# Last rows' attention scores as four 64x64 products, later pairs' scores in three float32r passes, and one PSUM pool kept for both phases

## Chip, core, metric

One core of one Trainium2 chip runs the whole program: an attention block and two mixture-style feed-forward layers, all in float32. The metric is the device time of one execution in microseconds. Engine names are those of the profile: PE is TensorE, PEld its weight loads, DVE VectorE, ACT ScalarE, POOL GpSimd, SP the engine that issues most DMAs.

## What is computed

```
# q, k, v: (4, 8, 576, 64); s: (4, 8, 576)
scores = scale * q @ k.T
cum = cumsum(max(s, 0));  bias = -(cum[:, None] - cum[None, :])
scores = where(causal, -1e9, scores + min(bias, 0))
scores -= max(scores);  attn = exp(scores);  attn /= sum(attn) + 1e-9
x = (attn @ v) as 2304 tokens x 512
h = x @ w1_in;  x = max(0.01 * h, h) @ w1_out        # 512 -> 2048 -> 512
h = x @ w2_in;  out = softplus(h) @ w2_out           # 512 -> 2048 -> 512
```

The causal mask leaves only keys at or before the query, where the bias is never above 0, so `min(bias, 0)` changes nothing that counts. The term `-cum[query]` is the same for a whole row and falls away when the row's maximum is taken off; only `+cum[key]` matters to the result, up to a constant of the row.

## The kernel before

**Attention.** Thirty-two (batch, head) maps are worked off as 16 pairs of heads `p` (four pairs per batch). Head 0 of a pair lies on partitions 0 to 63 of `Q`, `K` and so on, head 1 on partitions 64 to 127. The 576 queries are four blocks of 128 rows (`t` = 0 to 3) and a rest of `TL` = 64 rows. A pair has four units, in this order: block 3 (512 keys), the last 64 rows (all 576 keys, written `[]`), block 2 (384 keys), and blocks 1 and 0 together (256 and 128 keys).

`Unit.scores` makes the scores on PE. For the blocks, each product is made per head on 64 partitions (the two heads use the upper and lower half of the array's rows): a float32 product of `Q` and `K`, then a float32r product of `BQ` and `BK`, whose few non-zero rows hold the running sums `cum` in two parts and so add the decay (L286). For the last rows, both heads go through the whole array at once (L276): `Q` carries the 64 rows of head 0 and head 1 side by side with zeros in between, so that 128 output rows come out, in two halves of 288 keys, each a float32 product and a float32r decay product. The first pair has its decay in float32 (`BQ0`, `BK0`, shown as `PB` in the trace).

Then, per unit and head: `maxima` on DVE adds the mask and finds the row maximum (L305); `exps` on ACT (L319); `divisors` on DVE (L325, L326); `norm` on POOL (L330); `transpose` on PE (L347; the last rows L342 and L338); `evacuate` on ACT (L359) or DVE (L361); and `pv` on PE, which multiplies by V, the two heads on the two halves of the array's columns (L378), split into `xh` and `xl` on ACT and DVE (L385, L389).

The loop over units is written out by hand: in step `n`, scores of unit `n+1`, maxima and exponentials of `n`, norms of `n-1`, transposes of `n-2`. `i` is the step within a pair. Each engine takes its instructions in program order. `tick` and `later` put small follow-up work some half steps on.

**Fill.** From the second batch on, PE gets other work in between: `Fill` makes the first of four slices of the first layer for the tokens that are ready, in three chunks of `FW` = 512 columns (L143 and L583), half a unit per step, and stores the partial result (`part`). It also loads and splits weights (`load_w`, `split_w`: three DVE, three ACT and two POOL instructions each, L106 to L131), some of them in the first batch already.

**Feed-forward.** Every float32 product is made of three float32r products of high and low parts (`h_mm` L143, `out_mm` L709). The rest of the first slice goes over `first`, two chunks of 384 columns. After attention the PSUM pool `psA` closes, and the pools `ps_o` and `ps_h` open in its place. Stores and loads between the phases are on SP's queue, in program order.

Of the kernel before, what the change touches and what calls it, by code (L numbers as in the profile page):

```python
# [2 lines left out]

# [14 lines left out]
P = 128  # L18
# [12 lines left out]
def attn_moe_moe(ctx, tc, q, k, v, s, w1i, w1o, w2i, w2o, out):  # L31
# [12 lines left out]
    TL = S - NB * P  # L44
    FW = 512
    scale = 1.0 / float(D) ** 0.5
# [12 lines left out]
    xl = keep.tile([P, KD, NT], F32R, tag="xl", name="xl")  # L59
    bb_d = dram.tile([B * H, 2, S], F32R, tag="bb_d", name="bb_d")  # L60
    part = dram.tile([B - 1, P, KD, FW], F32, tag="part", name="part")

# [90 lines left out]
    def attention(att, ps, fills):  # L153
# [3 lines left out]

        ZQ = NB * P + 2 * TL
        own = [[slice(0, NB * P + TL)], [slice(0, NB * P), slice(NB * P + TL, ZQ)]]
        two = lambda nm, shape, dt=F32: [att.tile(shape, dt, tag=f"{nm}{i}", name=f"{nm}{i}") for i in range(2)]  # L160
        Q, K = two("Q", [P, ZQ]), two("K", [P, S])
        BQ, BK = two("BQ", [P, ZQ], F32R), two("BK", [P, S], F32R)
        V = two("V", [P, NB + 1, 2, D])
# [12 lines left out]
        def blank(i):  # L176

            bq = BQ[i].bitcast(F32)
            nc.gpsimd.memset(bq, 0.0)
            for j in range(2):  # L180
                for c in own[j]:
                    nc.gpsimd.memset(bq[j * D:j * D + 2, c], 1.0)

        def wake(x):

            pt = ps.tile([P, 512], F32, tag="a", name="pt_w", bufs=1)
            for i in range(8):
                nc.tensor.matmul(pt[:, :P], x, x, start=True, stop=True)

        def decay0():  # L190

            pitch = list(s1.ap[0])[0]
            nc.sync.dma_start(
                bass.AP(s1.tensor, s1.offset, [[D * pitch, 2], [1, S]]), bass.AP(s.tensor, s.offset, [[S, 2], [1, S]])
            )
            load(0, "q", nc.scalar)
            nc.sync.dma_start(c0, s.rearrange("b h s -> (b h) s"))
            load(0, "k", nc.scalar)
# [12 lines left out]
            nc.scalar.activation(BQ0[32:33, :S], BK0[:1], AF.Copy)  # L211
            n = 0
            for c, queue in zip(own[1], (nc.vector, nc.gpsimd)):
                m = n + c.stop - c.start
                queue.tensor_copy(BQ0[D + 32:D + 33, c], BK0[D:D + 1, n:m])
                n = m

# [6 lines left out]
        def parts():  # L224
            nc.vector.tensor_tensor(lo.bitcast(F32R), c1, hi, op=ALU.subtract)
            for e, x in enumerate((hi, lo)):
                nc.sync.dma_start(bb_d[:, e, :].bitcast(F32), x)

        def zeros():
# [5 lines left out]

        def load(p, nm, queue=nc.sync):
            if p < NP:
                t, x = {"q": (Q, q), "k": (K, k), "v": (V, v)}[nm]
                queue.dma_start(t[p % 2], x[p])

        def rows(p):

            if p < NP:
                b, hs = heads(p)
                for j in range(2):
                    h, r = b * H + hs.start + j, j * D
                    move(BK[p % 2][r:r + 2], bb_d[h])
                    n = 0
                    for c in own[j]:
                        m = n + c.stop - c.start  # L250
                        move(BQ[p % 2][r + 32:r + 34, c], bb_d[h, :, n:m])
                        n = m


        class Unit:
            def __init__(self, p, ts):
                self.p, self.ts = p, ts
                self.last = not ts
                o = 0
                self.subs = []  # L260
                for t in ts:
                    self.subs.append((t, slice(o, o + (t + 1) * P)))
                    o += (t + 1) * P
                self.W = S // 2 if self.last else o
                self.n = 1 if self.last else 2 * len(ts)

            def scores(self):
                i = self.p % 2
                bq, bk = (BQ[i], BK[i]) if self.p else (BQ0, BK0)
                ops = (Q[i], K[i]), (bq, bk)  # L270
                self.ps = [ps.tile([P, 512], F32, tag=f"s{j}", name="pt_s", bufs=2) for j in range(2)]
                if self.last:

                    for j, pt in enumerate(self.ps):
                        for x, y in ops:
                            nc.tensor.matmul(  # L276
                                pt[:, :self.W], x[:, NB * P:], y[:, j * self.W:(j + 1) * self.W],
                                start=x is Q[i], stop=x is bq,
                            )
                    return  # L280

                for t, c in self.subs:
                    for x, y in ops:
                        for j in range(2):
                            r = slice(j * D, (j + 1) * D)
                            nc.tensor.matmul(  # L286
                                self.ps[j][:, c], x[r, t * P:(t + 1) * P], y[r, :(t + 1) * P],
                                start=x is Q[i], stop=x is bq,
                            )
# [4 lines left out]
            def maxima(self, j):  # L294
                if j == 0:
# [4 lines left out]
                w = slice(0, self.W)  # L300
                todo = [(w, (mask[:, w], maskl)[j], j)] if self.last else [
                    (c, mask[:, (NB - 1 - t) * P:], j * len(self.subs) + i) for i, (t, c) in enumerate(self.subs)
# [120 lines left out]
        decay()  # L423
        fill.step(-2)
        load(1, "q")
        load(1, "k")
# [12 lines left out]
        for n in range(len(units) + 3):  # L439
# [48 lines left out]
    class Fill:  # L488
        def __init__(self, ps):
# [15 lines left out]
            def begin():  # L505

                with_o.__exit__(None, None, None)
                self.gpool, self.tpool = new("gpoolA", G + 1), new("tpoolA", 2)

# [39 lines left out]
        def h(self, f, x, gs):  # L549
            ps = self.bank("ps_h")  # L550
            h_mm(ps, 0, f, *x, range(KD // 2))
            new = lambda pool, nm, dt=F32: pool.tile([P, FW], dt, tag=nm, name=nm)

            def leaky():
                gf = new(self.tpool, "gf")
                nc.scalar.activation(gf, ps, AF.Prelu, alpha=0.01)
                later(1, high, gf)
# [17 lines left out]
        def o(self, dm, c, gs):  # L575
            ps = self.bank("ps_o")
            w = slice(dm * P, (dm + 1) * P)
# [18 lines left out]

    with pool("psA", bufs=2, space=PSUM) as psA:
        fills = []

        def make():  # L600
            fills.append(Fill(psA))
            return fills[0]

        with pool("att") as att:
            attention(att, psA, make)
        fill = fills[0]
        while fill.units or fill.rest or todo:
            fill.run()
            tick()
        fill.stack.close()  # L610

# [80 lines left out]
    def out_mm(n):  # L692
# [6 lines left out]
        for i in range(n_out):  # L699
            if f == 0:  # L700
                outs[i] = ps_o.tile([P, 512], F32, tag="o", name="ps_out")
        for i in range(n_out):
# [44 lines left out]
    for n, (layer, g, c, is_first, is_last, f) in enumerate(steps):  # L747
        N = c[1]
        cols = slice(c[0], c[0] + N)
        ps = ps_h.tile([P, 512], F32, tag="h", name="ps_h")  # L750
        h_mm(ps[:, :N], layer, g * G + f, xh[:, :, cols], xl[:, :, cols])
# [18 lines left out]
def lay_out(name, a):  # L770
# [9 lines left out]
    if name == "v":  # L780
# [3 lines left out]
        return r  # L784
    r = np.zeros((B * H // 2, 2, D, S + (tl if name == "q" else 0)), a.dtype)
    r[..., :S] = a.transpose(0, 1, 3, 2)
    if name == "q":
        r[:, 1, :, S:] = r[:, 1, :, n * P:S]
        r[:, 1, :, n * P:S] = 0
    return r.reshape(-1, 2 * D, r.shape[-1])  # L790

# [19 lines left out]
```

## Time and profile before

| | us |
|---|---|
| median of three runs | 986.3 (the others 985.24 and 1078.37) |
| the profiled execution | 985.13 |
| its span | 983.4 |
| PE busy | 973.2 (99%) |
| PE weight loads busy | 797.1 (81%) |
| DVE / ACT / POOL busy | 529.2 / 537.6 / 568.5 |
| chain that ended last: PE's share | 95% |

Attention fills the first quarter of the span, to about 254 us; the rest is feed-forward. A PE instruction's listed time holds its latency, and the next one starts while it runs, so what a piece of work costs PE is read from start to start. A float32 product stands as two records in the trace, a float32r product as one. The granted TensorE clock is 1.00 in every window.

### The profile page before, as it was taken

The page shows a single profiled execution, that of the slowest core. Times are in us where ns is not written, and L with a number is a line of the kernel's source. Part 1 is how long each engine was busy: PE and PEld are TensorE (multiplying, and loading weights), DVE is VectorE, ACT ScalarE, POOL GpSimd, SP SyncE. Part 2 cuts the span into 40 slices and gives each one's busy share as a digit, 9 for nine tenths or more (in the row PEclk, how much of TensorE's full clock was granted, in tenths as well). Part 3 has the DMA queues.
Part 4 walks back from the last instruction along what each step waited for, and adds up shares of the span by engine and source line. Part 5 has one row for each costly group of instructions (what it writes and reads, how often), then busy time and mean ns, then how long its engine had stood idle before and what let it go on. Part 6 is the DMA issues. An engine that isn't in the chain of part 4 may idle for free.

```text
span 983.4 us, 14578 instructions
## 1 busy us (share of the span) xinstructions
PE 973.2 (99%) x5226; PEld 797.1 (81%) x5226; DVE 529.2 (54%) x1139; ACT 537.6 (55%) x1119; POOL 568.5 (58%) x553
## 2 busy tenths in 40 slices
PE   8999999999999999999999999999999999999998
PEld 5767777777898888888888888888888888888886
DVE  7976666555121322232226347767587858764434
ACT  6887667656454333334335456776656555654452
POOL 7766456444264455345535546777777777874554
PEclk9999999999999999999999999999999999999999
DMA  6322331310540111011101210112011101100202
GB/s 200 123 102 81 125 122 63 111 52 25 178 134 22 52 56 43 22 48 60 43 22 44 65 43 22 43 44 64 23 44 43 59 27 44 44 1 1 86 22 86
DMA packets 35239, 61.20 MB, mean 62 GB/s; under 512 B 2566, under 2 KB 19718, under 8 KB 35168
## 3 DMA queue, kind: packets, MB, share of 16 engines
q1 hardware_dynamic: 34736, 59.53, 18.4%
q8 instruction: 41, 0.67, 0.3%
q10 hardware_dynamic: 432, 0.75, 0.2%
q14 instruction: 30, 0.25, 0.1%
HBM read 52.26 MB, written 8.01 MB: 61 GB/s over the span
## 4 chain that ended last, share of the span: by engine, by line
PE 95%; DVE 2%; ACT 1%; POOL 1%; issue 0%; DMA 0%; DVEq 0%; ACTq 0%; POOLq 0%
PE ps_h L143 40%; PE ps_out L709 37%; PE pt_v L378 4%; PE pt_s L286 4%; PE pt_t L347 3%; PE ps_o L583 3%; PE pt_s L276 2%; PE pt_t L342 1%; POOL sc L330 1%; ACT sc L319 1%; DVE sc L305 0%; DMA sc<-in_s 0%; POOL wm L121 0%; DVE acc L724 0%; DVE wm L118 0%
## 5 line engine op out<-in xcount | busy, mean ns | idle before, releaser
L149 POOL TENSOR_TENSOR gl<-gf,gh 128x512 fp32r<-128x512 f32 (+2 forms) x148 | 183.1, 1237 | 151.3 <-ACT gh L148 141.7
L143 PE MATMUL ps_h<-xh,wih 128*128 128x512 f32 (+2 forms) x640 | 237.7, 371 | 0.7 <-ACT o L587 0.7
L143 PE MATMUL ps_h<-xh,wil 128*128 128x512 f32 (+2 forms) x640 | 235.7, 368 | 0.0
L143 PE MATMUL ps_h<-xl,wih 128*128 128x512 f32 (+2 forms) x640 | 235.7, 368 | 0.0
L724 DVE TENSOR_TENSOR acc<-ps_out,acc 128x512 f32<-128x512 f32 (+1 forms) x115 | 73.8, 658 | 164.1 <-PE ps_out L709 164.1
L674 POOL TENSOR_TENSOR t<-e,t 128x512 f32<-128x512 f32 (+1 forms) x80 | 112.3, 1404 | 72.1 <-DVE t L673 71.3
L330 POOL TENSOR_SCALAR sc<-sc,st 128x512 f32<-128x512 f32 (+4 forms) x160 | 87.6, 560 | 96.7 <-DVE st L326 83.5
L143 PEld LDWEIGHTS ps_h<-xh,wih 128*128 128x128 f32 x640 | 120.6, 188 | 20.4 <-ACT o L587 1.2
L143 PEld LDWEIGHTS ps_h<-xh,wil 128*128 128x128 f32 x640 | 120.5, 188 | 19.6
L143 PEld LDWEIGHTS ps_h<-xl,wih 128*128 128x128 f32 x640 | 120.7, 189 | 19.1
L658 ACT ACTIVATE gf<-ps_h 128x512 f32<-128x512 f32 (+2 forms) x68 | 37.2, 547 | 178.1 <-PE ps_h L143 174.1
L148 ACT ACTIVATE gh<-gf 128x512 fp32r<-128x512 f32 (+2 forms) x148 | 86.1, 581 | 49.2 <-DVE gf L684 48.5
L709 PE MATMUL ps_out<-woh,gl 128*128 128x512 f32 x288 | 112.4, 390 | 0.0
L709 PE MATMUL ps_out<-woh,gh 128*128 128x512 f32 x288 | 112.3, 390 | 0.0
L709 PE MATMUL ps_out<-wol,gh 128*128 128x512 f32 x288 | 112.3, 390 | 0.0
L121 POOL TENSOR_TENSOR wm<-wm,wt 128x512 int32<-128x512 int32 x64 | 84.9, 1327 | 30.7 <-DVE wm L118 30.7
L319 ACT ACTIVATE sc<-sc,st 128x512 f32<-128x512 f32 (+2 forms) x144 | 83.5, 585 | 29.4 <-DVE st L325 22.8
L709 PE MATMUL ps_out<-gh,wol 128*128 128x512 f32 (+2 forms) x272 | 99.1, 364 | 0.0
L709 PE MATMUL ps_out<-gh,woh 128*128 128x512 f32 (+2 forms) x272 | 99.1, 364 | 0.0
L709 PE MATMUL ps_out<-gl,woh 128*128 128x512 f32 (+2 forms) x272 | 99.0, 364 | 0.0
L673 DVE TENSOR_SCALAR t<-e 128x512 f32<-128x512 f32 (+1 forms) x80 | 44.3, 553 | 98.4 <-ACT e L664 98.4
L112 DVE TENSOR_SCALAR wm<-wm 128x512 f32<-128x512 f32 x64 | 38.3, 599 | 95.6 <-ACT wm L106 95.4
(107 smaller groups left out, 1704.9 us busy)
## 6 DMA issues: line engine op xcount, KB each, us to landing
rawi<-in_moe_w_in SPq DMA_DIRECT2D x32, 512.0 KB
rawo<-in_moe_w_out SPq DMA_DIRECT2D x32, 512.0 KB
V<-in_v SPq DMA_DIRECT2D x16, 320.0 KB
Q<-in_q SPq DMA_DIRECT2D x15, 320.0 KB
out<-acc SPq DMA_DIRECT2D x17, 256.0 KB
K<-in_k SPq DMA_DIRECT2D x15, 288.0 KB
part<-o SPq DMA_DIRECT2D x12, 256.0 KB
acc<-part SPq DMA_DIRECT2D x3, 1024.0 KB
```

What stands on the lines that cost most here:

```text
L121: nc.gpsimd.tensor_tensor(m, m, t, op=ALU.add)
L143: nc.tensor.matmul(ps, a, b, start=kk == 0 and n == 0, stop=kk == KD - 1 and n == 2)
L148: nc.scalar.activation(gh, gf, AF.Copy)
L149: nc.gpsimd.tensor_tensor(gl, gf, gh.bitcast(F32), op=ALU.subtract)
L286: nc.tensor.matmul(self.ps[j][:, c], x[r, t * P:(t + 1) * P], y[r, :(t + 1) * P], start=x is Q[i], stop=x is bq,)
L319: nc.scalar.activation(x, x, AF.Exp, scale=-1.0, bias=self.stat(0, e), accum_out=self.stat(1, e))
L330: nc.gpsimd.tensor_scalar(x, x, self.stat(2, e), 1.0, op0=ALU.mult, op1=ALU.mult)
L378: nc.tensor.matmul(pt[j * D:(j + 1) * D, o:o + w], V[p % 2][:, c, j, :], x[:, j, :], start=m == 0 or (not last and m == 1), stop=m == len( ...
L673: nc.vector.tensor_scalar(t, e, 1.0, -1.0, op0=ALU.add, op1=ALU.add)
L674: nc.gpsimd.tensor_tensor(t, e, t, op=ALU.subtract)
L709: nc.tensor.matmul(ps, a, b, start=f == 0 and m == 0, stop=f == G - 1 and m == 2)
L724: nc.vector.tensor_tensor(d[..., x], o[..., x], d[..., x], op=ALU.add)
```

## The change

Five edits that hang together:

- **Last rows.** `Q` no longer holds zeros; the 64 last queries of the two heads are stored a second time with the heads swapped, and so are 288 keys of each head in `K` (864 columns now, 576 before). The scores are four float32 products of 64 rows by 64 columns of the array and 288 keys, one per quadrant of the array, with no decay product except for the first pair.
- **Decay of the last rows by DVE.** `decays` loads `cum` of the two heads, spread over 64 partitions each, into `M` (a DMA of 128 x 576 and one of 128 x 1, from the new DRAM tile `c_d`); `bias` takes off one column and adds the mask's 64 columns. `M` then stands in the place of the mask in `maxima`.
- **Three passes.** From pair index 7 on, blocks 3, 2 and 1 are made of three float32r products (`QH KH`, `QH KL`, `QL KH`) in place of one float32 product. `split` makes the parts a pair ahead: per operand one ACT copy and one DVE subtraction of 128 x 512.
- **Chunks of 448** columns in the fill, and `first` becomes two chunks of 480; some fill pools have one buffer fewer.
- **PSUM pool kept.** `psA` stays open; the feed-forward phase takes its banks by name (three for `ps_h`, five for `ps_out`, as many as before).

Also: the loads of `Q` and `K` are issued a step earlier in the pair and two pairs ahead, the decay rows (`rows`) come in four DMAs of 512 columns, not five, and the program starts with 12 dummy products, not 8.

```diff
-    FW = 512
+    FW = 448
...
-            for i in range(8):
+            for i in range(12):
...
+        def decays(p):
+
+            if p < NP:
+                o = c_d.offset + p * 2 * S
+                nc.sync.dma_start(M[:, :S], bass.AP(c_d.tensor, o, [[S, 2], [0, D], [1, S]]))
+                nc.sync.dma_start(M[:, S:S + 1], bass.AP(c_d.tensor, o + SB, [[S, 2], [1, TL], [1, 1]]))
+
+        def bias(p):
+            if 0 < p < NP:
+                nc.vector.tensor_scalar(M[:, :S], M[:, :S], M[:, S:S + 1], None, op0=ALU.subtract)
+                nc.vector.tensor_tensor(M[:, SB:S], M[:, SB:S], maskl[:, SH - TL:], op=ALU.add)
+
+
+        PARTS = 2 * NPAIR - 1
+
+        def split(p, h, l, x):
+
+            if PARTS <= p < NP:
+                h, l, x = h[p % 2], l[p % 2], x[p % 2][:, :SB]
+                nc.scalar.activation(h, x, AF.Copy)
+                later(1, lambda: nc.vector.tensor_tensor(l, x, h.bitcast(F32), op=ALU.subtract))
...
-                ops = (Q[i], K[i]), (bq, bk)
+                ops = [(Q[i], K[i]), (bq, bk)]
+                few = [(QH[i], KH[i]), (QH[i], KL[i]), (QL[i], KH[i]), (bq, bk)] if self.p >= PARTS else ops
...
-                    for j, pt in enumerate(self.ps):
-                        for x, y in ops:
+                    for e in range(2):
+                        for j, pt in enumerate(self.ps):
+                            r, o = (slice(h * D, (h + 1) * D) for h in (j, j ^ e))
+                            x, y = (S, S) if e else (SB, j * SH)
                             nc.tensor.matmul(
-                                pt[:, :self.W], x[:, NB * P:], y[:, j * self.W:(j + 1) * self.W],
-                                start=x is Q[i], stop=x is bq,
+                                pt[o, :SH], Q[i][r, x:x + TL], K[i][r, y:y + SH], start=True, stop=self.p > 0
+                            )
+                    if not self.p:
+                        for j, pt in enumerate(self.ps):
+                            nc.tensor.matmul(
+                                pt[:, :SH], bq[:, SB:], bk[:, j * SH:(j + 1) * SH], start=False, stop=True
                             )
...
-                    for x, y in ops:
+                    for m, (x, y) in enumerate(few if t else ops):
...
             if i == 0:
+                bias(p)
                 if p:
-                    load(p + 1, "q")
-                    load(p + 1, "k")
                     rows(p + 1)
+            elif i == 1:
+                split(p + 1, QH, QL, Q)
+            elif i == 2:
+                split(p + 1, KH, KL, K)
+                decays(p + 1)
+            else:
+                load(p + 2, "q")
+                load(p + 2, "k")
...
-    with pool("psA", bufs=2, space=PSUM) as psA:
-        fills = []
...
+    psA = ctx.enter_context(pool("psA", bufs=2, space=PSUM))
+    fills = []
...
-    ps_o = ctx.enter_context(pool("ps_o", bufs=5, space=PSUM))
-    ps_h = ctx.enter_context(pool("ps_h", bufs=3, space=PSUM))
+    banks = {
+        "ps_h": cycle((("t", 2), ("t", 2), ("a", 1))),
+        "ps_out": cycle((("m", 1), ("s0", 2), ("s0", 2), ("s1", 2), ("s1", 2))),
+    }
```

PE's order at pair index 8, from block 3's scores to the last rows' scores; `pt_s` are scores, `pt_t` transposes of an earlier unit, `ps_o` fill. Before:

```order
L286 MATMUL pt_s<-K_86,Q_84 128x512 x2
L286 MATMUL pt_s<-BK_90,BQ_88 128x512 x2
L342 MATMUL pt_t<-ident,sc 128x128 x4
...
L338 MATMUL pt_t<-ident,sc 64x128
L276 MATMUL pt_s<-K_86,Q_84 128x288
L276 MATMUL pt_s<-BK_90,BQ_88 128x288
L276 MATMUL pt_s<-K_86,Q_84 128x288
L276 MATMUL pt_s<-BK_90,BQ_88 128x288
```

Now, at the same place:

```order
L311 MATMUL pt_s<-KH_98,QH_94 128x512 x2
L311 MATMUL pt_s<-KL_100,QH_94 128x512 x2
L311 MATMUL pt_s<-KH_98,QL_96 128x512 x2
L311 MATMUL pt_s<-BK_91,BQ_89 128x512 x2
L368 MATMUL pt_t<-ident,sc 128x128 x4
...
L364 MATMUL pt_t<-ident,sc 64x128
L297 MATMUL pt_s<-K_87,Q_85 64x288 x4
```

Two float32 products of block 3 became six float32r products, and the four products of the last rows over the whole array became four over a quarter of it each; the neighbours are the same.

DVE's order at pair index 7, from the end of block 3's maxima to block 2's; `pt_t` copies are evacuations, `xl` belongs to `pv`. Before:

```order
L326 RECIPROCAL st<-st 128x4
L305 ISA sc,st<-pt_s,mask 128x512
...
L389 TENSOR_TENSOR xl<-pt_v,xh 128x192
L305 ISA sc,st<-pt_s,maskl 128x288
...
L361 COPY PB<-pt_t 128x3x128
L305 ISA sc,st<-pt_s,mask 128x384
...
L326 RECIPROCAL st<-st 128x1
L305 ISA sc,st<-pt_s,mask 128x384
```

Now, at the same place:

```order
L352 RECIPROCAL st<-st 128x4
L260 TENSOR_SCALAR M<-M 128x576
L261 TENSOR_TENSOR M<-M,maskl 128x64
L331 ISA sc,st<-pt_s,mask 128x512
...
L415 TENSOR_TENSOR xl<-pt_v,xh 128x192
L271 TENSOR_TENSOR QL_96<-Q_85,QH_94 128x512
L331 ISA sc,st<-pt_s,M 128x288
...
L352 RECIPROCAL st<-st 128x1
L271 TENSOR_TENSOR KL_100<-K_87,KH_98 128x512
L331 ISA sc,st<-pt_s,mask 128x384
```

Each of the three steps has new DVE work ahead of the second head's maxima: two instructions of `bias` in every pair but the first, and one subtraction in each of two steps from pair index 6 on.

## Rows read from the trace of the kernel before

**Rows 1.** The page: busy us of each engine, share of the span, instructions.
```profile
PE 973.2 (99%) x5226; PEld 797.1 (81%) x5226; DVE 529.2 (54%) x1139; ACT 537.6 (55%) x1119; POOL 568.5 (58%) x553
```
**Rows 2.** Who PE waited for, whole span: us in total, times, longest us.
```profile
PE pt_t L347 <- POOL sc L330: 1.0, 3, 0.5
PE ps_h L143 <- ACT o L587: 0.7, 1, 0.7
```
**Rows 3.** Windows of one pair each: length, busy us of PE, PEld, DVE, ACT, POOL, clock, DMA.
```profile
28.89:39.67 10.78, 10.78 (x94) 7.94 (x92) 10.37 (x41) 9.99 (x30) 8.58 (x13) 1.00 0.42 142
39.67:50.44 10.77, 10.77 (x93) 7.95 (x92) 9.58 (x39) 9.33 (x26) 7.58 (x12) 1.00 0.41 139
50.44:62.97 12.53, 12.05 (x94) 8.25 (x92) 11.24 (x39) 9.92 (x30) 8.10 (x12) 1.00 0.24 79
...
79.30:95.64 16.34, 16.34 (x117) 12.26 (x116) 10.68 (x38) 12.32 (x32) 12.13 (x16) 1.00 0.23 78
...
110.61:126.94 16.33, 16.33 (x117) 12.25 (x116) 10.03 (x39) 10.74 (x29) 8.20 (x13) 1.00 0.39 125
```
**Rows 4.** The chain of waits in the first 64 us: start, us, what.
```profile
26.86 0.66 PE pt_t L347 x4
...
46.71 0.49 ACT PB L359
...
60.93 0.66 PE pt_t L347 x4
```
**Rows 5.** PE's timeline, first pair, float32 decay of the last rows: start, us, what.
```profile
8.44 0.65 PE L276 MATMUL pt_s<-PB 128*128 128x288 f32 x2
8.92 0.65 PE L276 MATMUL pt_s<-K,Q 128*128 128x288 f32 x2
```
**Rows 6.** PE's timeline, feed-forward, twelve float32r products of 512 columns.
```profile
300.09 0.39 PE L709 MATMUL ps_out<-gh,woh 128*128 128x512 f32 x1
...
302.81 0.39 PE L143 MATMUL ps_h<-xh,wih 128*128 128x512 f32 x1
```
**Rows 7.** PE's timeline of one pair: block 3, the last rows, and what follows each.
```profile
190.89 1.13 PE L286 MATMUL pt_s<-K,Q 64*128 64x512 f32 x4
...
192.18 0.66 PE L342 MATMUL pt_t<-ident,sc 128*128 128x128 f32 x4
...
194.16 0.65 PE L276 MATMUL pt_s<-K,Q 128*128 128x288 f32 x2
...
195.41 0.49 PE L347 MATMUL pt_t<-ident,sc 128*128 128x128 f32 x3
```
**Rows 8.** The timeline of the same pair: `pv` of 192 columns, then block 2.
```profile
197.54 1.52 PE L378 MATMUL pt_v<-PA,V 128*64 128x192 f32 x16
...
199.10 0.92 PE L286 MATMUL pt_s<-K,Q 64*128 64x384 f32 x4
...
200.13 0.55 PE L347 MATMUL pt_t<-ident,sc 128*128 128x128 f32 x3
```
**Rows 9.** Single lines: duration in ns, min/median/max, then first and last start.
```profile
L112 DVE TENSOR_SCALAR wm<-wm x64: 410/428/1365, 10.9 to 873.0; 128x512 f32<-128x512 f32 x64
L310 DVE TENSOR_TENSOR st<-st x16: 158/612/1307, 12.7 to 233.0; 128x1 f32<-128x1 f32 x16
L646 DVE TENSOR_TENSOR xl<-acc,xh x20: 411/684/1778, 519.1 to 599.4; 128x512 fp32r<-128x512 f32 x16, 128x256 fp32r<-128x256 f32 x4
L125 ACT ACTIVATE wih<-wm x32: 617/632/636, 16.9 to 862.8; 128x512 fp32r<-128x512 f32 x32
```
**Rows 10.** The timeline of DVE and ACT in one pair's step of block 2.
```profile
187.23 0.62 ACT L319 ACTIVATE sc<-sc,st 128x384 f32<-128x384 f32 x1 [1.59 <-DVE st L325]
...
187.32 0.54 DVE L305 CUSTOM_DVE_ANT_0 sc<-pt_s,mask 128x384 f32<-128x384 f32 x1
```
**Rows 11.** The timeline from attention to feed-forward, on DVE and PE.
```profile
253.84 0.56 DVE L389 TENSOR_TENSOR xl<-pt_v,xh 128x384 fp32r<-128x384 f32 x1 [4.20 <-ACT xh L385]
...
255.58 0.44 PE L143 MATMUL ps_h<-xh,wih 128*128 128x384 f32 x1 [0.74 <-ACT o L587]
```

More of the change, by code (lines that the diff above doesn't have):

```diff
@@ L2 @@
 from contextlib import ExitStack
+from itertools import cycle
 import concourse.bass as bass
@@ L154, in attention @@
         ident = att.tile([P, P], F32, tag="ident", name="ident")
-        ZQ = NB * P + 2 * TL
-        own = [[slice(0, NB * P + TL)], [slice(0, NB * P), slice(NB * P + TL, ZQ)]]
+        SB, SH = NB * P, S // 2
+        ZQ, ZK = S + TL, S + SH
         two = lambda nm, shape, dt=F32: [att.tile(shape, dt, tag=f"{nm}{i}", name=f"{nm}{i}") for i in range(2)]
-        Q, K = two("Q", [P, ZQ]), two("K", [P, S])
-        BQ, BK = two("BQ", [P, ZQ], F32R), two("BK", [P, S], F32R)
+        Q, K = two("Q", [P, ZQ]), two("K", [P, ZK])
+        BQ, BK = two("BQ", [P, SB], F32R), two("BK", [P, SB], F32R)
+        M = att.tile([P, S + 32], F32, tag="M", name="M")
+        QH, QL, KH, KL = (two(nm, [P, SB], F32R) for nm in ("QH", "QL", "KH", "KL"))
         V = two("V", [P, NB + 1, 2, D])
@@ L197, in decay0 @@
             nc.sync.dma_start(c0, s.rearrange("b h s -> (b h) s"))
-            load(0, "k", nc.scalar)
+            load(0, "k", nc.scalar, slice(0, S))
             nc.vector.memset(one[:, :P], 1.0)
@@ L211, in decay0 @@
             nc.scalar.activation(BQ0[32:33, :S], BK0[:1], AF.Copy)
[L212 to L216, printed above, removed]
+            for c, n, queue in ((slice(0, SB), 0, nc.vector), (slice(S, ZQ), SB, nc.gpsimd)):
+                queue.tensor_copy(BQ0[D + 32:D + 33, c], BK0[D:D + 1, n:n + c.stop - c.start])
         hi, lo = one[:BH], c0
@@ L246, in rows @@
                     h, r = b * H + hs.start + j, j * D
[L247 to L252, printed above, removed]
+                    move(BK[p % 2][r:r + 2], bb_d[h, :, :SB])
+                    move(BQ[p % 2][r + 32:r + 34], bb_d[h, :, :SB])
+        def decays(p):
[13 more added lines that the diff above has]
+                later(1, lambda: nc.vector.tensor_tensor(l, x, h.bitcast(F32), op=ALU.subtract))
         class Unit:
@@ L263, in __init__ @@
                     o += (t + 1) * P
-                self.W = S // 2 if self.last else o
+                self.W = SH if self.last else o
                 self.n = 1 if self.last else 2 * len(ts)
@@ L300, in maxima @@
                 w = slice(0, self.W)
-                todo = [(w, (mask[:, w], maskl)[j], j)] if self.last else [
+                ml = (mask[:, w], maskl)[j] if not self.p else M[:, j * SH:(j + 1) * SH]
+                todo = [(w, ml, j)] if self.last else [
                     (c, mask[:, (NB - 1 - t) * P:], j * len(self.subs) + i) for i, (t, c) in enumerate(self.subs)
@@ L424, in attention @@
         fill.step(-2)
+        load(0, "k", nc.sync, slice(S, None))
         load(1, "q")
@@ L507, in begin @@
                 with_o.__exit__(None, None, None)
[L508 removed]
+                self.gpool, self.tpool = new("gpoolA", G), new("tpoolA", 2)
             self.begin = begin
@@ L549, in h @@
         def h(self, f, x, gs):
-            ps = self.bank("ps_h")
+            ps = self.bank("ps_h")[:, :FW]
             h_mm(ps, 0, f, *x, range(KD // 2))
@@ L554, in leaky @@
             def leaky():
-                gf = new(self.tpool, "gf")
+                gf = self.tpool.tile([P, FW], F32, tag="gf", name="gf", bufs=1)
                 nc.scalar.activation(gf, ps, AF.Prelu, alpha=0.01)
@@ L575, in o @@
         def o(self, dm, c, gs):
-            ps = self.bank("ps_o")
+            ps = self.bank("ps_o")[:, :FW]
             w = slice(dm * P, (dm + 1) * P)
@@ L595, in o, with make @@
             self.rest = rest
-    with pool("psA", bufs=2, space=PSUM) as psA:
-        fills = []
[L600 to L610, printed above, removed]
+    psA = ctx.enter_context(pool("psA", bufs=2, space=PSUM))
+    fills = []
+    def make():
+        fills.append(Fill(psA))
+        return fills[0]
+    with pool("att") as att:
+        attention(att, psA, make)
+    fill = fills[0]
+    while fill.units or fill.rest or todo:
+        fill.run()
+        tick()
+    fill.stack.close()
     wpools.append(ctx.enter_context(pool("wpool1", bufs=2)))
@@ L622, in attn_moe_moe, with bank @@
     tpool = ctx.enter_context(pool("tpool", bufs=2, side="right"))
-    ps_o = ctx.enter_context(pool("ps_o", bufs=5, space=PSUM))
-    ps_h = ctx.enter_context(pool("ps_h", bufs=3, space=PSUM))
+    banks = {
+        "ps_h": cycle((("t", 2), ("t", 2), ("a", 1))),
+        "ps_out": cycle((("m", 1), ("s0", 2), ("s0", 2), ("s1", 2), ("s1", 2))),
+    }
+    def bank(nm):
+        tag, bufs = next(banks[nm])
+        return psA.tile([P, 512], F32, tag=tag, name=nm, bufs=bufs)
     chunks = [(0, 512), (512, 512), (1024, NT - 2048), (NT - 1024, 512), (NT - 512, 512)]
@@ L700, in out_mm @@
             if f == 0:
-                outs[i] = ps_o.tile([P, 512], F32, tag="o", name="ps_out")
+                outs[i] = bank("ps_out")
         for i in range(n_out):
@@ L749, in attn_moe_moe @@
         cols = slice(c[0], c[0] + N)
-        ps = ps_h.tile([P, 512], F32, tag="h", name="ps_h")
+        ps = bank("ps_h")
         h_mm(ps[:, :N], layer, g * G + f, xh[:, :, cols], xl[:, :, cols])
@@ L784, in lay_out @@
         return r
-    r = np.zeros((B * H // 2, 2, D, S + (tl if name == "q" else 0)), a.dtype)
-    r[..., :S] = a.transpose(0, 1, 3, 2)
+    a = a.transpose(0, 1, 3, 2)
     if name == "q":
-        r[:, 1, :, S:] = r[:, 1, :, n * P:S]
-        r[:, 1, :, n * P:S] = 0
-    return r.reshape(-1, 2 * D, r.shape[-1])
+        more = a[:, ::-1, :, n * P:]
+    else:
+        more = np.stack([a[:, 1, :, :S // 2], a[:, 0, :, S // 2:]], 1)
+    return np.concatenate([a, more], -1).reshape(B * H // 2, 2 * D, -1)
 def kernel(**inputs):
```

11 lines of the change are left out of this document (6 added, 5 removed).

## The prediction

> **What bounds the kernel now.** Read first the page's busy line [rows 1]: PE is busy for 99% of the span, no other engine for 60%. A busy PE may still hide gaps, so look next at what PE waited for [rows 2]: its two longest entries add up to 1.7 us. Then comes the table by pair [rows 3], in which a window reaches from one pair's first scores to the next pair's. In the pairs with full fill (16.33 and 16.34 us) PE is busy throughout, DVE for at most 10.7 and ACT for at most 12.3 us in the windows shown. There, what PE is spared is time saved. The first batch has no fill and is another matter: at pair index 2 the pair takes 10.78 us with DVE busy for 10.37, and at index 4 it takes 12.53 us, of which PE is idle for 0.48. The chain of waits says the same [rows 4]: it runs on PE from 26.86 to 46.71 us, then on ACT, DVE and POOL until 60.93, and on PE from there to the end of attention; before 26.86 it runs on ACT, DVE and POOL too. So the change is worth its PE time from pair index 5 on, which is 11 pairs, and little ahead of it.
>
> **PE's prices, from start to start.** A float32 product over the whole array takes 8.92 - 8.44 = 0.48 us for 288 columns [rows 5] (two records are one product), 1.67 ns a column. Twelve float32r products of 512 columns take 302.81 - 300.09 = 2.72 us [rows 6], 0.227 us each: 0.417 ns a column and 13 ns fixed. Block 3, with a float32 and a float32r product of 512 columns per head, takes 192.18 - 190.89 = 1.29 us [rows 7]; block 2, with 384 columns, 200.13 - 199.10 = 1.03 [rows 8]. The difference is 0.26 us for 128 columns, 2.03 ns a column. One head alone needs 1.67 + 0.42 = 2.09, so the second head costs nothing: the two halves of the array's rows work side by side. What is left of block 3 is fixed: 1.29 - 512 x 2.09 ns = 0.22 us. `pv` [rows 8] has per head four float32 products of 192 columns and one of 64: 832 x 1.67 ns = 1.39 us, and takes 199.10 - 197.54 = 1.56. So two heads on the halves of the array's columns go side by side too, with 0.17 us fixed.
>
> **Last rows.** Now 195.41 - 194.16 = 1.25 us [rows 7] (15 pairs agree within 0.01): two float32 products and two float32r ones, one after another. Afterwards four float32 products of 288 columns, one per quadrant. If all four run side by side they need 0.48 us, and I add 0.20 us fixed, between the 0.17 of `pv` and the 0.22 of block 3, since the neighbours on PE (transposes over the whole array) are of another shape, as there. That makes 0.68, a gain of 0.57 us. Bounds: 0.77 with nothing fixed; and where only two of the four run side by side, 2 x 0.48 + 0.20 = 1.16, a gain of 0.09. Rows show side by side by array rows and by columns, each alone, and never both at once; I take four, as nothing in either case shows a limit. The Trainium skill, TensorEngine Tiling (Array Packing), section Tiling Modes, lists 64x64 as four independent tiles; its section Key Properties says that a change of tiling mode drains the engine, which would speak against this edit. No row here shows four quadrants at once; the fixed 0.17 and 0.22 us are what such a drain may cost in this trace. Gain: 11 x 0.57 = 6.3 us.
>
> **Three passes.** Per pair 512 + 384 + 256 = 1152 columns go from 1.67 to 3 x 0.417 = 1.25 ns: 0.48 us. The float32 product came as two records and now there are three products, so each block also pays for one more pair of fixed 13 ns and of weight loads: 0.03 us a block at least. I take a gain of 0.40 us a pair, between 0.45 and 0.25 (where the 256-column passes wait for weights). Nine pairs: 3.6 us.
>
> **Chunks of 448.** The number of fill products stays at 3 x 96 = 288; each loses 64 columns: 288 x 64 x 0.417 ns = 7.7 us leave attention, and 192 products of `first` gain 96 columns each: 7.7 us come back in feed-forward. The sum is nothing as long as PE sets the pace in both places; the pools with one buffer fewer hold data for at most one chunk, and by the order of the code a new chunk asks for its first buffer only after PE has read the old one, so I cost them at nothing.
>
> **PSUM pool kept.** Feed-forward's first product starts at 255.58 us after 0.74 us of waiting for the last `ps_o` to leave the old pool, while `xl`, its last input, was done at 253.84 + 0.56 = 254.40 [rows 11]. With the banks taken by name that wait goes: 0.7 us. Next in line would be `xl`, which is earlier; the range is 0 to 1.0.
>
> **Work for DVE, ACT and SP.** `bias` is an instruction of 128x576 and one of 128x64. The nearest rows [rows 9] are L112 (0.41 us at best, 0.43 median, 1.37 at worst for 512) and L310 (0.16, 0.61, 1.31 us for a single element): 0.62 to 2.7 us, and I take 0.75, near the undisturbed ends, as the bulk lies in the first. `split` is an ACT copy (L125, 0.63 us) and a DVE subtraction (L646, 0.68 median, 1.78 worst), each twice a pair. With fill they go beside PE: at pair index 8 DVE has 10.03 us of 16.33 and would get 0.75 + 1.4, ACT 10.74 and would get 1.3 [rows 3], against a PE that then needs 16.34 - 0.57 - 0.40 - 24 x 64 x 0.417 ns = 14.7 us. What the waits do to the order: DVE's subtraction stands ahead of the second head's maxima and waits for a copy which stands behind an exponential on ACT. In block 2's step that exponential ends at 187.85 us, so the copy ends near 188.7, the subtraction near 189.4, the maxima near 189.9 in place of 187.86 [rows 10]; PE wants the bank and the parts at 190.89 [rows 7]. A microsecond of cover, then, less what PE runs ahead. On SP, `M` needs two DMAs a pair and `K` grows by half, while `rows` loses one DMA; they stand ahead of the weight loads in their step, and their users come two steps later, so I cost them at nothing.
>
> In the first batch there is no cover: at index 2 DVE would need 10.37 + 0.75 = 11.1 us, 0.35 more than the pair takes now; at index 3 it would need 9.58 + 0.75 = 10.3 of the 10.77, so that some 0.15 us may be gained; at index 1 and 4 PE's gain is not on the chain and some of DVE's work is, 0.3 us each. Together a loss of 0.8 us; bounds: a gain of 4 x 0.57 = 2.3, a loss of 4 x 0.75 = 3.0.
>
> **Sum.** -6.3 - 3.6 - 0.7 + 0.8 = -9.8 us. The profiled execution took 985.13, so 975.3; from the median of 986.3 it is 976.5. I say **976 us**, 1.0% less.
>
> **Rivals.**
> 1. *Two by two.* The quadrants that share array rows don't overlap in this mode: 11 x 0.09 = 1.0 in place of 6.3, about 981. Against it stands `pv`, whose products share all rows. Chance 0.10.
> 2. *Late feeds.* DVE's subtractions and `bias` run into POOL, PE waits in some steps, and half the gain of pairs 5 to 15 goes: about 980 to 983. For it: L310 takes 0.16 to 1.31 us for one element, so DVE is held up by something else. The Trainium skill, SBUF — State Buffer, Who interferes with whom, says that a DVE instruction with two SBUF inputs and a GpSimd instruction reading SBUF lock each other out; the spread of L310 agrees. Against it: at index 2 DVE is 96% busy and PE still goes without a wait. Chance 0.12.
> 3. *Slower.* The same feeds become the pace of attention, so that pairs with fill keep near 16.3 us. Then the shorter fill saves nothing in attention, and its 7.7 us are still paid in feed-forward: 985.1 + 7.7 - 0.7 + 0.8 = 993 at worst. It turns to a loss from the point where the pair stays above 15.6 us, since 11 x 0.7 is the price of the moved columns; PE alone would want 14.7. Index 4 shows such a pair, at 12.53 us where PE has 12.05. About 989; chance 0.06.
> 4. *More.* The first batch gains as well, and the quadrants cost nothing fixed: -8.5 - 4.0 - 1.0 - 1.5 = -15, about 970. Chance 0.07.
>
> **Numbers.** The forecast, 973 to 979, has 0.65. The range from 971 to 983.5 takes in the first two rivals and leaves the third and most of the fourth out. 2% is 19.7 us and about what a measurement of this kernel can tell from no change; no case reaches it, so I leave 0.04 for faster and 0.02 for slower.
>
> **What would show it.** Last rows: PE from the first 64x288 product to the next transpose, 0.68 us (1.16 under the first rival). Block 3 near 1.10, block 2 near 0.89. A pair with fill near 14.8 us from index 7 on, near 15.1 at 5 and 6, and PE still without waits there; under rivals 2 and 3 PE waits for DVE or POOL at transposes and scores. Pair index 2 near 11.1. No wait at feed-forward's first product. I am wrong if quadrants are slow, if the parts come late, or if the kernel's start gets longer because the last 288 columns of `K` come behind a weight load.

## The result, and the profile after

The changed kernel takes **998.4 us** (median of 5, 997.89 to 999.55) against 986.3: a ratio of 1.0127, 95% interval 1.0112 to 1.0142. It is 1.3% slower, where I had forecast 976 us and a range of 971 to 983.5. The ratio compares fast executions alone and leaves out the one of 1078.37 us of the kernel before, so it is not the quotient of the two medians. Of the profiled execution's 997.89 us the span is 996.1.

The page after, first the busy line, then the chain of waits by engine; it answers to [rows 1]:

```profile
PE 978.1 (98%) x5322; PEld 798.5 (80%) x5322; DVE 548.7 (55%) x1187; ACT 543.8 (55%) x1137; POOL 574.6 (58%) x551
...
PE 87%; DMA 6%; DVE 3%; ACT 2%; SPq 0%; issue 0%; DVEq 0%; ACTq 0%
```

The busy shares hardly differ from before. The chain is what gives the change away: 6% of it, 56 us in six pieces of 9.0 to 9.8 us, is one load, `M<-c_d`. The waits of the whole span (us in total, times, longest) show the same; before, PE's longest entries were 1.0 and 0.7 us [rows 2]:

```profile
DVE M L260 <- DMA M<-c_d: 13.1, 10, 2.9
...
PE pt_s L311 <- DVE st L331: 6.8, 8, 2.0
```

DVE stands at `bias` (L260) until `M` has landed, the second head's maxima (L331) stand behind it, and PE's next scores (L311) wait for the bank that these maxima read. By pair (columns as in [rows 3]; these are pair indices 1, 2, 3, 4, 8 and 13):

```profile
15.84:32.96 17.12, 13.47 (x95) 8.93 (x94) 13.12 (x48) 11.36 (x32) 11.62 (x15) 0.90 0.42 110
32.96:49.20 16.24, 14.43 (x95) 9.62 (x93) 10.85 (x40) 9.86 (x27) 8.47 (x13) 0.79 0.50 127
49.20:60.19 10.99, 10.87 (x96) 7.53 (x94) 9.06 (x36) 9.11 (x26) 7.59 (x12) 1.00 0.60 167
60.19:74.61 14.42, 12.46 (x96) 7.83 (x94) 11.48 (x40) 9.65 (x30) 8.37 (x12) 1.00 0.52 134
...
122.91:140.72 17.81, 16.23 (x125) 12.09 (x123) 12.69 (x42) 11.26 (x32) 8.52 (x12) 1.00 0.52 133
...
201.99:216.85 14.86, 14.86 (x126) 11.69 (x124) 10.53 (x40) 9.99 (x29) 5.36 (x10) 1.00 0.45 129
```

Pair index 2 takes 16.24 us where it took 10.78 [rows 3]. In the first two windows PE stands still, from 23.9 to 25.8 and from 39.0 to 40.7 us; afterwards, from 27.0 to 30.4 and from 40.7 to 47.5 us, the granted clock is at the lower of its two levels (1.2 in place of 2.4 GHz), which makes 0.90 and 0.79 on the mean of the windows, and products there take longer. Index 8 takes 17.81 us in place of 16.33 [rows 3]. Only late pairs such as index 13 have the forecast length, 14.86 against 14.8. The chain of the first 43 us (start, us, what) shows what sets the pace at the start:

```profile
14.06 0.59 SPq L255
...
14.69 9.62 DMA M<-c_d
...
24.41 0.53 DVE M L260
...
28.16 0.36 DVE sc L331
...
28.56 0.52 SPq L255
...
29.12 9.75 DMA M<-c_d
...
38.96 0.80 DVE M L260
...
42.50 0.36 DVE sc L331
...
42.90 0.52 SPq L255
```

This is a loop. There is one buffer `M`: SP may issue the next load only when the maxima of this pair's last rows have read it, the load takes 9.6 us, DVE prepares it and reads it, and only then may SP issue again. (The row of 9.62 us begins with the issue of the column's load, right behind that of `M` at 14.06; which of the two is late, e2 tells below.) From issue to issue it is 14.50 and 14.34 us, and pairs that took 10.8 us [rows 3] cannot run faster than that on average: indices 1 to 4 take 58.77 us, 14.7 each, though index 3, whose first scores came late, takes only 10.99. From 14.06 to 84.41 us no piece of this chain is on PE.

PE's prices came out as forecast. PE's timeline of pair index 12, which answers to [rows 7]:

```profile
186.57 0.50 PE L311 MATMUL pt_s<-KH,QH 64*128 64x512 f32 x2
...
187.70 0.66 PE L368 MATMUL pt_t<-ident,sc 128*128 128x128 f32 x4
...
189.62 0.71 PE L297 MATMUL pt_s<-K,Q 64*64 64x288 f32 x8
190.27 0.55 PE L373 MATMUL pt_t<-ident,sc 128*128 128x128 f32 x3
```

Block 3 in three passes takes 187.70 - 186.57 = 1.13 us (forecast 1.10, before 1.29), the last rows 190.27 - 189.62 = 0.65 (forecast 0.68, before 1.25).

Why most of these 9.6 us are needed is in the DMA view. From 43 to 49 us hardly anything but `M` is in flight; the digits are the busy share of the 16 engines in tenths, in slices of 0.175 us:

```profile
DMA  0000005000000011110111011011111101996698
GB/s 12 0 0 0 0 0 26 0 26 26 26 13 26 26 53 53 53 53 39 53 53 53 39 53 53 39 53 53 53 53 53 53 39 53 98 155 82 69 97 82
DMA packets 134, 0.31 MB, mean 44 GB/s; under 512 B 2, under 2 KB 2, under 8 KB 134
```

A digit of 1 is 1.6 to 3.2 engines out of 16, and while it stands the rate is 53 GB/s at most. At that rate the 0.31 MB take some 6 us, an estimate from this view; what the flight holds ahead of the first packet and behind the last it does not explain. The source of this load has an outer dimension of 2, `[[S, 2], [0, D], [1, S]]`. The Trainium skill, DMA: Bandwidth & Descriptors, section Why a DMA increments its semaphore by 16 and not by 1, says that the number of engines is the largest one up to 16 that divides the slowest dimension of both sides of the transfer; these are 2 and 128 here, which makes 2 engines, and the digits of 1 agree. My prediction overlooked it.

### The profile page after: what moved, and what is told of

Its sections match the earlier page's. It is cut to its first block, busy times and chain, and to the rows that moved or that the text cites. A ratio compares the mean times of both kernels' runs of the same rounds, so it can differ in the third digit from the quotient of the medians.

```text
span 996.1 us, 14924 instructions
## 1 busy us (share of the span) xinstructions
PE 978.1 (98%) x5322; PEld 798.5 (80%) x5322; DVE 548.7 (55%) x1187; ACT 543.8 (55%) x1137; POOL 574.6 (58%) x551
## 3 DMA queue, kind: packets, MB, share of 16 engines
q1 hardware_dynamic: 38768, 65.57, 22.4%
## 4 chain that ended last, share of the span: by engine, by line
PE 87%; DMA 6%; DVE 3%; ACT 2%; SPq 0%; issue 0%; DVEq 0%; ACTq 0%
PE ps_h L145 40%; PE ps_out L749 37%; DMA M<-c_d 6%; PE pt_v L404 3%; PE pt_s L311 3%; PE pt_t L373 2%; PE ps_o L617 2%; ACT sc L345 1%; DVE sc L331 1%; PE pt_w L191 1%; DVE M L260 0%; PE pt_t L368 0%; PE pt_s L297 0%; DVE QL L271 0%; SPq L255 0%
## 5 line engine op out<-in xcount | busy, mean ns | idle before, releaser
L145 PE MATMUL ps_h<-xh,wih 128*128 128x512 f32 (+3 forms) x640 | 237.7, 371 | 0.4 <-ACT gf L590 0.3
L145 PE MATMUL ps_h<-xh,wil 128*128 128x512 f32 (+3 forms) x640 | 235.7, 368 | 0.0
L145 PE MATMUL ps_h<-xl,wih 128*128 128x512 f32 (+3 forms) x640 | 235.7, 368 | 0.0
L356 POOL TENSOR_SCALAR sc<-sc,st 128x512 f32<-128x512 f32 (+4 forms) x160 | 92.7, 591 | 99.3 <-DVE st L352 71.3
```

Source lines behind the costliest of these rows:

```text
L145: nc.tensor.matmul(ps, a, b, start=kk == 0 and n == 0, stop=kk == KD - 1 and n == 2)
L356: nc.gpsimd.tensor_scalar(x, x, self.stat(2, e), 1.0, op0=ALU.mult, op1=ALU.mult)
```

## The experiments

Three theories stood at first. **T1**: few DMA engines serve the load of `M`, it is late, and DVE and PE wait. **T2**: the load of the 128x1 column behind it is what is late. **T3**: DVE's added work and the splits cost the time, whatever the DMA does. Every kernel is the changed one with the edit named; ratios are to the kernel before, with 95% intervals.

| run | edit | median us | ratio |
|---|---|---|---|
| e1 | one load of `M` for each head | 982.0 | 0.9966 (0.9953 to 0.9979) |
| e2 | no column, no subtraction | 990.5 | 1.0044 (1.0029 to 1.0058) |
| e3 | no three passes | 995.0 | 1.0093 (1.0076 to 1.0110) |
| e4 | e3, two buffers `M`, load two steps earlier | 985.9 | 1.0004 (0.9994 to 1.0013) |
| e5 | e1 and e3 | 981.0 | 0.9952 (0.9936 to 0.9969) |
| e6 | e1, splits earlier | 980.1 | 0.9944 (0.9929 to 0.9959) |
| e7 | e1 and e2 | 980.0 | 0.9942 (0.9928 to 0.9957) |
| e8 | e1, 8 products in `wake` | 982.0 | 0.9966 (0.9953 to 0.9979) |
| e9 | one load of `M` for each half of the columns | 995.2 | 1.0099 (1.0084 to 1.0115) |
| e10 | e6 and e2 | 978.6 | 0.9931 (0.9917 to 0.9946) |
| e11 | e5, chunks of 512 | 980.8 | 0.9957 (0.9946 to 0.9967) |
| e12 | e10, three passes for six pairs only | 978.1 | 0.9928 (0.9913 to 0.9943) |

**e1, one load for each head.**

```diff
-nc.sync.dma_start(M[:, :S], bass.AP(c_d.tensor, o, [[S, 2], [0, D], [1, S]]))
+for j in range(2):
+    nc.sync.dma_start(M[j * D:(j + 1) * D, :S], bass.AP(c_d.tensor, o + j * S, [[0, D], [1, S]]))
```

> The load of `M` is issued as two DMAs, one for each head (64 partitions by 576 each), in place of one whose source has an outer dimension of 2; the column's load stays. T1 (the one DMA of `M` is served by few of the DMA engines and lands 9 to 9.7 us after its issue; VectorE waits for it at `bias`, and TensorE behind VectorE): `M` lands within about 4 us, VectorE's waits at `bias` for `M` (13.1 us in 10 of them) fall to under 2 us, the pairs of the first batch lose 10 to 12 us, and the time is 980 to 988. T2 (the load of the 128x1 column is what is late): no change, 996 to 1000. T3 (VectorE's added work in the first batch, the splits' queueing, or the shorter fill cost the time, whatever the DMA does): the waits may shrink, but the time stays above 992.

Measured 982.0 us, 16.3 less than the changed kernel. DVE no longer waits for `M` at `bias` at all. Pair indices 1 to 4 are 9.7 us shorter together (T1: 10 to 12), and 5 to 9 another 5.3. That `M` lands within 4 us no row shows; in pair 1 DVE uses it 7.1 us after the first issue, without a wait. The windows of pair indices 1 and 2, and the DMA view from 38 to 41 us (slices of 0.075 us; the two loads are issued between 37.85 and 38.95):

```profile
15.97:30.32 14.35, 11.92 (x94) 7.54 (x93) 13.30 (x43) 10.83 (x31) 11.22 (x15) 1.00 0.53 171
30.32:41.37 11.05, 11.01 (x95) 7.49 (x93) 10.32 (x41) 9.65 (x30) 8.72 (x13) 1.00 0.47 155
```

```profile
DMA  0000000000000049208795733336567646256939
GB/s 0 0 0 0 0 0 0 0 0 0 0 0 0 0 61 123 31 0 184 154 246 215 154 154 154 154 123 246 215 246 307 246 154 185 62 155 189 161 96 130
DMA packets 268, 0.31 MB, mean 104 GB/s; under 512 B 134, under 2 KB 134, under 8 KB 268
```

The same 0.31 MB now goes by in some 2 us, mostly at 3 to 9 tenths, and the granted clock is back at 1.00. T1 holds for 16.3 of the 22.4 us by which I was wrong.

**e2, no column.** The load of the column and the first instruction of `bias` are left out.

> Leaves out the load of the 128x1 column and VectorE's subtraction of it (a constant of each row, which the softmax takes out again); the load of `M` stays one DMA. T1: `M` still lands some 6 us after its issue, the column's 3 us behind it are gone, and so is one VectorE operation of 0.5 us a pair; the waits at `bias` halve and the time is 986 to 993. T2: the waits at `bias` vanish and the time is 980 to 986. T3: 992 to 998, the 0.5 us a pair of VectorE at most.

Measured 990.5. The size fits T1's range, but not by its reasoning: the column is gone and the other load still needs 10 us from its issue, as the chain shows, so it had never waited for the column.

```profile
41.54 9.92 DMA M<-c_d
54.67 10.10 DMA M<-c_d
```

What the edit shortens is the rest of the loop, now 54.67 - 41.54 = 13.1 us: an issue on SP and a DVE instruction of 0.52 us are gone. The waits at `bias` did not halve: they are 12.6 us in 6. T2 falls.

**e3 and e4, the load covered.** e3 sets `PARTS = NP`, so that no pair takes three passes. e4 adds a second buffer and issues the same slow load earlier:

```diff
-        M = att.tile([P, S + 32], F32, tag="M", name="M")
+        Ms = two("M", [P, S + 32])
...
                 if p:
+                    decays(p + 1)
                     rows(p + 1)
...
-                decays(p + 1)
+                if not p:
+                    decays(1)
```

> Every pair keeps its scores in fp32: no three passes from the eighth pair on, no splits on ScalarE and VectorE. T1: `M` is as late as in the changed kernel, and only the three passes' gain is lost: 998 to 1002. T3 in the form that the splits' queueing on VectorE costs the time: faster than the changed kernel, 988 to 995.

> The kernel without three passes, and with two buffers for `M`, whose one DMA is issued a pair earlier (at the first step of the pair before, in place of its third). The DMA itself is unchanged. T1: it lands as slowly, but before VectorE asks for it; the waits at `bias` vanish but for the first pair's, and the time is 8 to 12 us under the kernel without three passes. If the slow DMA hurts by what it delays behind it on the same engines, and not by VectorE's wait, the gain is under 5 us. T3: no change against the kernel without three passes.

Measured 995.0 and 985.9: 9.1 us for a load that is no faster but has a pair's time to land. Its first use is not covered, and DVE still waits 4.0 us for it in pair 1, which takes 19.3 us between the first scores; every later pair is within 0.2 us of its length in e5. So the slow transfer harms by the wait at its end and not by what it delays on the DMA engines. e3 was a surprise: without the three passes the kernel is 3.4 us faster, where T1 wanted 998 to 1002. It lies at the upper end of what T3 gave for the splits (988 to 995), so T3 holds for a part; e5 takes that up.

**e9, two loads of half the columns.** It tells the outer dimension from the number of loads:

```diff
-nc.sync.dma_start(M[:, :S], bass.AP(c_d.tensor, o, [[S, 2], [0, D], [1, S]]))
+for x in (0, SH):
+    nc.sync.dma_start(M[:, x:x + SH], bass.AP(c_d.tensor, o + x, [[S, 2], [0, D], [1, SH]]))
```

> The changed kernel with the load of `M` as two DMAs again, but cut the other way: each loads half of the columns (288) of both heads, so that its source keeps the outer dimension of 2. D (the outer dimension of 2 decides on how many of the DMA engines serve a load): the DMA share stays near a tenth while they run, VectorE waits for `M` as in the changed kernel, and the time is 995 to 1001. N (it is the number of DMAs that decides, two being served side by side): 980 to 986, as with one DMA for each head.

Measured 995.2. From 28 to 40 us (the loads are issued from 27.68 on) the share stays at a tenth for some 3 us and the rate at 46 GB/s or less, and DVE's wait for `M` is there again:

```profile
DMA  0001111111111001100117559999996969989989
GB/s 0 0 0 35 42 46 46 38 38 42 42 38 31 8 8 38 46 31 23 54 46 111 129 148 289 374 381 307 182 167 137 204 199 274 294 320 362 373 332 372
```

```profile
DVE M L261 <- DMA M<-c_d: 12.1, 5, 4.5
```

The outer dimension decides, not the number of loads; that one is worth 3.2 us at most, which is what e9 is below the changed kernel.

**e5, where the other 6 us are.** S: the splits take back what the passes save. P: the passes are worth 3.6 us and the loss is elsewhere. The edit is e1's and e3's together.

> The load of `M` as two DMAs, and no pair in three passes (no splits). With the two loads alone the time was 982.0 us, 6 over the forecast. S (the splits hold up VectorE and ScalarE at pair indices 7, 8 and 10 and take back what the three passes save): 980 to 982.5, and these three pairs get 0.4 to 1.3 us shorter while the undisturbed ones (9, 13, 14) get 0.35 longer. P (the passes are worth the forecast 3.6 us, and the 6 us are lost elsewhere): 985 to 986.

Measured 981.0, 1.05 us less than e1. The pairs of index 7, 8 and 13, first of e1 (three passes), then of e5 (float32 throughout):

```profile
95.46:110.91 15.45, 14.32 (x119) 10.86 (x118) 11.17 (x45) 11.79 (x33) 8.13 (x12) 1.00 0.40 121
110.91:126.80 15.89, 15.41 (x126) 11.76 (x125) 12.50 (x42) 11.37 (x32) 9.47 (x12) 1.00 0.46 149
...
186.86:201.72 14.86, 14.86 (x125) 11.70 (x123) 10.57 (x40) 10.01 (x29) 5.25 (x10) 1.00 0.51 154
```

```profile
94.88:109.03 14.15, 14.03 (x113) 10.34 (x111) 9.60 (x37) 9.06 (x26) 7.71 (x13) 1.00 0.37 105
109.03:124.54 15.51, 15.47 (x119) 11.41 (x117) 11.31 (x40) 10.62 (x29) 8.49 (x13) 1.00 0.46 150
...
184.12:199.34 15.22, 15.22 (x120) 11.40 (x118) 9.11 (x37) 8.87 (x26) 5.25 (x11) 1.00 0.49 167
```

At index 13 PE is busy throughout in both and the passes save 0.36 us. At index 7 PE is idle for 1.13 us of e1's pair and the pair is 1.30 longer. S holds. In the profiled executions e5 is 1.64 us shorter, 1.47 of it from index 7 to 14; another 0.57 lies in pair 1, which the edit does not touch.

**e6, the splits earlier.** `split` of `Q` and `K` one step earlier, and `later(2, ...)` in place of `later(1, ...)`.

> The load of `M` as two DMAs; the splits of `Q` and `K` one step earlier (first and second step of the pair in place of second and third), with VectorE's subtraction a whole step behind ScalarE's copy in place of half a step. S: VectorE's waits for the copies (7.6 us in 7) vanish, pairs 7, 8 and 10 fall to between 14.1 and 15.2 us, and the time is 978 to 980.5. P: VectorE's waits vanish too, but the time stays within 0.8 us of 982.0.

Measured 980.1, in S's range. DVE's wait for the copies, in e1

```profile
DVE KL L272 <- ACT KH L271: 7.6, 7, 1.6
```

is gone, as both had forecast: e6 has no such row, neither for `KL` nor for `QL`. Index 10 gained 0.76 us (14.86) and index 12 0.45, but index 8 only 0.30 (15.59, above S's range), 7 (15.02) did not reach the length without splits, and 11 became 0.34 longer (14.63). So that wait was a part of what the splits cost, not the whole. About 1 us of the gain lies ahead of pair index 5, where there are no splits, so it is not the edit's.

**e7, the subtraction in the first batch.** e1 and e2 together.

> The load of `M` as two DMAs, without the column and its subtraction (leaves out a constant of each row, which the softmax takes out again): 0.52 us a pair less on VectorE. B (in the first batch VectorE sets the pace, so that its added work there is paid): pairs 1 to 4 get 1.2 to 2.1 us shorter together, 979.5 to 981. Otherwise (its work is hidden there too): 981.5 to 982.5.

Measured 980.0, in B's range. Pairs 1 to 4 are 1.4 us shorter together than in e1, 0.6 of it at index 2 and 3, and 5 and 6 are as they were. But pair 1 is long in e1's profiled execution, 14.35 us; e5, e6 and e8, whose edits do not touch it, have 13.78, 13.86 and 13.77. Against e5 the four pairs are 0.8 us shorter: DVE's work is paid there, as B says, at less than B's size. Another 0.7 us comes at index 11, where splits run too, which B had not expected.

**e8, `wake`.** `range(8)` in place of `range(12)`.

> The load of `M` as two DMAs, and 8 products in `wake` as in the kernel before, in place of 12. W (the four added products keep TensorE from block 3 of the first pair until 6.46 us, where the kernel before began at 5.20): block 3 begins by 5.4 us, and as VectorE's first maxima began 0.7 us later, the time falls by 0.4 to 0.8 us, 981.2 to 981.6. If the start is bound by the work ahead on ScalarE, VectorE and GpSimd: no change, 981.7 to 982.3; if a shorter `wake` leaves TensorE with less than its full clock in the first pair: 982.5 to 985.

Measured 982.0, no change, though block 3 then begins at 5.43 us and not at 6.46. In the profiled execution (983.19, the longest of five) that lead is lost at once, as block 3's products take 3.78 us in the chain of e8, the first row here, and 2.14 in that of e1, the other two:

```profile
5.43 3.78 PE pt_s L312 x8
```

```profile
1.04 5.49 PE pt_w L191 x24
6.53 2.14 PE pt_s L312 x8
```

The chain of e1 begins on PE, with `wake` (`pt_w`), so it does not show a start that is bound by the work ahead on the other engines. Why block 3 is slower in e8 stays open: the granted clock reads 1.00 in both.

**e11, chunks.** e5 with `FW = 512`; the unused tiles of the parts (`QH` and so on) are left out, as in e4.

> The kernel with two loads and without three passes (981.0), with chunks of 512 columns as in the kernel before in place of 448. Z (as forecast, the columns cost TensorE the same in attention as in feed-forward): 980.3 to 981.7, the last `pv` some 6 to 8 us later and feed-forward as much shorter. If the shorter fill was no gain in attention: 974 to 978; if the longer fill collides with VectorE and ScalarE: over 982.

Measured 980.8, no change. The windows from the first scores to the last `pv` and from there to the end, of e5 and then of e11:

```profile
6.46:240.88 234.42, 230.13 (x1767) 167.02 (x1766) 169.54 (x628) 165.08 (x456) 136.55 (x203) 1.00 0.41 129
240.88:979.20 738.32, 734.59 (x3479) 617.95 (x3478) 363.67 (x532) 367.11 (x660) 429.02 (x332) 1.00 0.15 48
```

```profile
6.46:248.90 242.44, 238.31 (x1767) 167.07 (x1766) 171.82 (x627) 167.76 (x455) 138.06 (x202) 1.00 0.40 126
248.90:979.20 730.30, 726.55 (x3479) 615.61 (x3478) 364.79 (x532) 365.09 (x660) 427.21 (x332) 1.00 0.16 50
```

8.0 us leave one window and 8.0 come into the other: Z, and the forecast's term.

**e10 and e12, the best of it.** e10 is e6 without the column; e12 gives three passes only to the pairs of index 9, 10, 12, 13, 14 and 15.

> Load of `M` as one DMA for each head, earlier splits, no column and no subtraction of it (leaves out a constant of each row, which the softmax takes out again). Each of the last two took 1.9 to 2.0 us off the 982.0 alone. If they act in different places (pairs with splits, first batch): 977.5 to 979. If both only relieve VectorE at the same steps: 979.5 to 980.1.

> As the run with earlier splits and without the column, but three passes only at the pair indices 9, 10, 12, 13, 14 and 15, where the trace showed them 0.3 us shorter than in fp32; 7, 8 and 11, where they were 0.1 to 0.8 us longer, stay in fp32. S: 1 to 2 us less than the run with all nine pairs, 976 to 977.5. If the loss only moves to the next pair whose splits come first: no change, 978 to 979.

Measured 978.6 and 978.1, both 0.7% under the kernel before. The two edits of e10 together take 3.5 us off, of the 4.0 that they took one by one. e12 missed S's 976 to 977.5; 978 to 979 was the forecast for a loss that only moves. Index 7 is back at 14.16 us, but index 11, now in float32 itself, takes 14.72 where e5 has 13.98. Index 11 is where the splits for pair 12 run. So the time is lost in the pair that does the splits, though not in every one: index 8 does those for pair 9 and takes 15.52 where e5 has 15.51. Index 11 has three chunk units in place of four, so it is shorter and may hide less; that is read from the traces and was not tried by itself.

## Why the prediction was wrong

The miss is 998.4 - 976.0 = 22.4 us. By the runs it is 16.3 for the load of `M` (changed kernel against e1), 4.7 for the three passes (forecast 3.6 gained, measured 1.05 lost), and 1.4 that e5 is above what the forecast is without the passes (981.0 against 979.6). Of the 1.4, 0.5 is the rounding of 976.5 to 976, and the start may be more of it: the first scores of pair 1 come at 15.97 us in e5 and at 15.27 in the kernel before, where the forecast had nothing for 12 dummy products in place of 8. They come anywhere from 14.99 (e12) to 16.08 us (e2) in the traces with 12, so these runs give the start no firm price.

- **`M`'s loads on SP at nothing: the step that failed.** I wrote that their users come two steps later and costed them so, without asking how long the load flies, how many engines its shape gives it, or how long two steps are where there is no fill. By the chain it flies 9.6 us (10 us without the column, e2), and with one buffer it closes a loop of 14.3 us around pairs of 10.8.
- **Three passes.** The gain on PE was right, 0.36 us a pair where the splits are hidden (forecast 0.40). The cost of the splits was not: I allowed a microsecond of cover behind PE, from one full pair, and the pairs of index 7, 8 and 10 had less.
- **`bias` in the first batch.** +0.8 us was right once the load is out of the way: pairs 1 to 4 take 48.53 us together in e5 and 47.70 (15.27 to 62.97 us) in the kernel before, 0.83 more. By e7 the subtraction alone is about 0.8 us there.
- **Last rows** (0.65 us against 0.68), **chunks** (8.0 us out, 8.0 back) and the **PSUM pool** (PE is busy without a gap from 250 to 275 us, so the 0.74 us of [rows 11] are gone) were right. PE's pair of index 5 is 15.19 us in e5, forecast 15.1.
- **The rivals.** Two by two is refuted by 0.65 us. Late feeds comes nearest to the splits, but DVE waited there for ACT's copies (7.6 us in e1), not for POOL. The slower rival had the sign with another mechanism: it wanted DVE's work to pace the full pairs, while the pace was a DMA's latency, for the most part in the pairs without fill (9.7 us in pairs 1 to 4, 5.3 in 5 to 9). Among my signs of being wrong stood parts that come late; `M`, the load that did, I had nowhere.

Of the 16.3 us little can be the lower granted clock that followed the waiting, though e1 took away both. The chain is off PE from 14.06 to 84.41 us, which takes in both stretches of the lower clock. From issue to issue its turns take 14.50, 14.34, 13.76, 14.33 and 14.38 us: the first three hold those stretches, the last two have a granted clock of 1.00 throughout and are no shorter. And the 5.3 us of pairs 5 to 9 were lost at 1.00.

## What to carry to other kernels

Before a load is costed at nothing, set its flight time, as its own shape gives it, against the time from issue to first use in the shortest pair; with one buffer, flight, use and reissue make a loop, and pairs cannot be shorter than that loop on average. Work that hides beside a busy engine should be placed by the pair with the least cover, as some pairs here, 7 above all, paid for the splits that full ones such as 13 hid.

## What was not expected of the hardware

A broadcast to two groups of 64 partitions in one load went at about 50 GB/s, and as two loads of one group each mostly at 123 to 307 GB/s, for the same 0.31 MB. The Trainium skill, DMA: Bandwidth & Descriptors, section Rules for kernel authors, advises against splitting a transfer into partition halves; here it was worth 16.3 us, because the split takes away an outer dimension of 2, of which the same section warns. Four 64x64 float32 products at once, of which the trace of the kernel before shows none, take 0.65 us for 288 columns, from start to start, next to transposes over the whole array.
